# A new table of planned times for the first three units, and five small guards moved to GpSimd

## The chip, the cores and the metric

The kernel runs on one core of a Trainium2 chip. Its engines are TensorE (PE in the profile, with its weight loads as PEld), VectorE (DVE), ScalarE (ACT), GpSimd (POOL) and SyncE (SP), which here issues all the DMAs. Each engine works through its own queue strictly in order; between engines there are semaphores. The metric is the device time of one execution in microseconds (us). Before the change three runs took 532.4, 533.78 and 532.07 us, median 532.4.

## The reference

Two stages. Causal attention with a window of 64 positions, per head, and then a gated block with a convolution of three taps over the sequence:

```python
scores = scale * np.matmul(q, k.transpose(0, 1, 3, 2))       # B=8, H=8, S=576, D=64
mask = (rel >= 0) & (rel < window)                           # window = 64
scores = np.where(mask, scores, -1000000000.0)
scores = scores - np.max(scores, axis=-1, keepdims=True)
attn = np.exp(scores)
attn = attn / (np.sum(attn, axis=-1, keepdims=True) + 1e-09)
x = np.matmul(attn, v)                                       # then [B, S, 512]
h = np.maximum(x @ w_in, 0.0)                                # w_in [512, 1024]
for k in range(K):
    conv_out += conv_w[k][None, None, :] * hp[:, k:k + S, :]  # hp: h padded by one row
gate = 1.0 / (1.0 + np.exp(-conv_out))
out = (h * gate) @ w_out                                     # w_out [1024, 512]
```

The weights arrive as 64-bit floats and are turned into 32-bit ones on the chip.

## The kernel before

**Tiling.** The 8 x 576 positions are cut into twelve units of 384. Per unit the attention is worked off in three blocks `b` (scores in `qk`, L346; the windowed maximum in `row_max`, L361, eight instructions at L363; exponents with their sums in `exps`, L373; 1e-9 added to the sums in `guard`, L376; `reciprocal`, L379; `normalise`, L384). Then the weights of a block are transposed: by TensorE (L390) and copied out by ScalarE (L395) in units 0 and 1, by VectorE (L411) and 24 small DMAs (L423) from unit 2 on. `values` (L487) multiplies by v for four groups `c` of two heads into the two PSUM banks `acc`; ScalarE rounds the result to `xh` (L491), VectorE makes the rest `xl` (L494), so that three single-pass products stand for one in full precision.

**The two big products.** Per unit and per chunk `f` of 128 hidden features (eight of them), `mm1` makes h from x: 12 matmuls at L507, into `acc` banks too. ScalarE takes them out (L528), starts the convolution (L534), VectorE adds the two side taps (L541), ScalarE applies the sigmoid (L548), VectorE multiplies (L553), ScalarE rounds to `gh` (L557) and VectorE makes the rest `gl` (L561), for two chunks at a time. `mm2` adds up the output: 3 matmuls at L570 for each of four output banks `po`, so 12 for a chunk.

**Weights.** `weights` (L261) loads the bits of one chunk or of two (L267), and `to_f32` (L244) makes floats of them: ScalarE's absolute value of the high word (L248), a maximum with 2^-15 (L250 on VectorE for the first two chunks of w_in, which come singly; L252 on GpSimd for all others), two VectorE steps with the bits (L253, L255), ScalarE's scaling of the low word (L258), VectorE's addition (L259). Then the high part is copied, by GpSimd for w_in (L276) and by ScalarE for w_out (L274), and VectorE subtracts it (L277, into `wil` and `wol`). There are two buffers, `w240` and `w241` in the rows below; the single chunks lie in the halves of `w240`.

**What sets the order.** The whole program is a list of pieces of work, each with a planned time: `START` (L140) holds the numbers, counted in chunks (unit 0's first chunk is 0, the attention before it has negative numbers). For `qk`, `ex`, `pv` and `sig` the first row is used around unit 0, the second around unit 1, the third for all later units. `queued` (L61) walks through the list with a cost for each piece and puts onto each engine, at each step, that ready piece whose planned time is lowest. The order it finds is the order in which the instructions are issued. Where it finds TensorE without work it puts in matmuls on a spare tile (`keep_busy`, L207, at L212), a fixed number of them.

Of the kernel before, what the change touches and what calls it, by code (L numbers as in the profile page):

```python
# [12 lines left out]
ALU = mybir.AluOpType  # L13
# [20 lines left out]
TINY = 2.0 ** -15  # L34
# [26 lines left out]
def queued(works, fill=None):  # L61
# [76 lines left out]


START = {  # L140
    "v0": -27.5,
    "pv0": -15.968,
    "conv": -37.437,
    "bits": ((-46.561, -47.419), (-44.383, -45.007)),
    "qk1": -43.011,
    "v1": -11.849,
    "qk2": -2.185,
    "qk0": (-91.154, -52.794, -48.024),
    "ex0": (-42.377, -37.771, -19.993),
    "sc1": (-20.012, -18.408, -14.041),  # L150
    "ex1": (-8.106, -4.046, -3.778),
    "mask": -0.529,
    "sig": ((3.087, 7.079, 8.764, 10.751), (3.178, 6.73, 5.945, 9.966), (4.046, 6.806, 8.285, 10.314)),
    "in": (-39.031, -37.38, -33.878, -12.682, -12.013),
    "out": (-11.963, -8.679, 1.926, 7.315),
# [3 lines left out]
}  # L159
SWITCH = {"PE": 0.14, "ACT": 1.28}  # L160
LEAVE = 0.24
PORT_CL = 0.5
# [5 lines left out]
def attention_moe(ctx: ExitStack, tc: tile.TileContext, q, k, v, w_in, conv_w, w_out, out):  # L168
    nc = tc.nc
# [13 lines left out]
    mask = many(3, [P, P], F32, "mask")  # L183
# [13 lines left out]
    bits = [flat.bitcast(U32)[:, 4 * DM * i:4 * DM * (i + 1)].rearrange("p (e two) -> p e two", two=2) for i in range(2)]  # L197
# [20 lines left out]
    def at(t, eng, cost, do, r=(), w=(), kind=None, mb=0, port=0.0):  # L218

        plan.append(Work(t, eng, cost, do, list(r), list(w), kind, mb, port))  # L220

    def two(t, eng, cost, do, **kw):
        at(t, eng, cost, do, port=cost, **kw)
# [17 lines left out]

    def to_f32(t, n, st, x, kb, kt, early=False):  # L244

        lw, hw, xu = st[..., 0], st[..., 1], x.bitcast(U32)

        at(t, "ACT", 0.0009 * n + 0.2, lambda: nc.scalar.activation(x, hw.bitcast(F32), AF.Abs), r=kb, w=kt)  # L248
        if early:
            two(t, "DVE", 0.00052 * n + 0.06, lambda: nc.vector.tensor_scalar(x, x, TINY, None, op0=ALU.max), w=kt)  # L250
        else:
            at(t, "POOL", 0.0027 * n + 0.02, lambda: nc.gpsimd.tensor_scalar(x, x, TINY, None, op0=ALU.max), w=kt, port=PORT_CL)  # L252
        two(t, "DVE", 0.00052 * n + 0.06, lambda: nc.vector.tensor_scalar(  # L253
            xu, xu, 3, 0x3FFFFFF8, op0=ALU.logical_shift_left, op1=ALU.bitwise_and), w=kt)
        two(t, "DVE", 0.00104 * n + 0.07, lambda: nc.vector.scalar_tensor_tensor(  # L255
            xu, hw, 0xC0000000, xu, op0=ALU.bitwise_and, op1=ALU.bitwise_or), r=kb, w=kt)

        at(t, "ACT", 0.0009 * n + 0.2, lambda: nc.scalar.activation(lw, lw, AF.Copy, scale=2.0 ** -29), w=kb)  # L258
        two(t, "DVE", 0.00104 * n + 0.07, lambda: nc.vector.tensor_tensor(xu, xu, lw, ALU.add), r=kb, w=kt)  # L259

    def weights(t, src, fs, hi, lo, key, buf, halves):  # L261

        e = slice(halves[0] * DM, (halves[-1] + 1) * DM)
        st, x = bits[buf][:, e], w24[buf][:, e]
# [3 lines left out]
                bits[buf][:, a * DM:(a + 1) * DM], src[f].bitcast(U32).rearrange("p (e two) -> p e two", two=2)),  # L268
               w=[("bits", buf, a)], mb=0.52)
        n = len(fs) * DM  # L270
        to_f32(t, n, st, x, kb, kt, len(fs) == 1)
        his, los = [f"{key}{f}h" for f in fs], [f"{key}{f}l" for f in fs]
        if key == "out":
            at(t, "ACT", 0.0009 * n + 0.12, lambda: nc.scalar.copy(hi, x), r=kt, w=his)  # L274
# [159 lines left out]
    def softmax(u, b, t, ex_at):  # L434
# [7 lines left out]
        t = ex_at  # L442
# [2 lines left out]
               w=[("s", b, i), ("sm", b, i)], kind="exp")  # L445
        t += 0.45
        sw = [("sm", b, i) for i in range(NB)]
        if 0 < u < 3:
            at(t, "POOL", 0.6, lambda b=b: guard(b, nc.gpsimd), w=sw)
        else:  # L450
            at(t, "DVE", 0.15, lambda b=b: guard(b, nc.vector), w=sw)
# [285 lines left out]
```

## Time and profile before

| | us |
|---|---|
| median of three runs | 532.4 |
| lowest and highest | 532.07, 533.78 |
| the profiled execution | 530.72 |
| its span on the core | 528.9 |
| first product into the output banks (L570) starts at | 69.49 |
| last matmul group on the chain (L570) ends at | 524.92 |

The profiled execution was 1.7 us faster than the median of the runs. Its span begins with the first instruction and ends with the last one; 1.8 us of the execution lie outside of it. In rows of the timeline the first number is the start in us from the span's start, the second the length, then engine, line, operation, what is written from what, the shapes and the count; in brackets stands how long the engine was idle before it, and what ended that. The granted clock of TensorE was 0.999 of full speed.

### The profile page before, as it was taken

How to read it: one execution, taken by the hardware profiler on the slowest of the kernel's cores; microseconds unless marked ns; L12 is line 12 of the kernel's file. 1: busy time of each engine (PE TensorE's matmuls, PEld its weight loads, DVE VectorE, ACT ScalarE, POOL GpSimd, SP SyncE). 2: the span in 40 equal slices, each digit the busy share in tenths (PEclk: the TensorE clock that was granted, in tenths of full speed). 3: DMA queues.
4: the chain of work that ended last, by engine and by line, in shares of the span. 5: the costliest groups of instructions: out<-in, count | busy, mean ns of one | idle time of the engine just before them, and what ended most of it. 6: DMA issues, size and time to landing. Idle time of an engine off the chain costs nothing.

```text
span 528.9 us, 14823 instructions
## 1 busy us (share of the span) xinstructions
PE 518.7 (98%) x5824; PEld 499.8 (94%) x5824; DVE 376.7 (71%) x1089; ACT 382.1 (72%) x1015; POOL 96.9 (18%) x187
## 2 busy tenths in 40 slices
PE   9999799999999999999999999999999999999996
PEld 8898799999899999999999999999999999999996
DVE  4899999964958677667767767767767667655552
ACT  2999889549896696696697687687687687544542
POOL 5253452103031011021021021021021021000000
PEclk9999999999999999999999999999999999999999
DMA  8992570235283273172182174183074053010011
GB/s 281 352 318 100 195 277 23 68 122 198 75 314 81 78 252 78 48 289 74 26 295 71 24 245 122 27 287 99 14 270 118 14 150 103 20 61 0 2 60 62
DMA packets 29462, 69.98 MB, mean 132 GB/s; under 512 B 5712, under 2 KB 17616, under 8 KB 29392
## 3 DMA queue, kind: packets, MB, share of 16 engines
q1 hardware_dynamic: 29392, 69.03, 39.4%
q8 instruction: 46, 0.75, 0.6%
q14 instruction: 24, 0.20, 0.1%
HBM read 47.73 MB, written 9.47 MB: 108 GB/s over the span
## 4 chain that ended last, share of the span: by engine, by line
PE 87%; DVE 7%; DMA 2%; SPq 1%; ACT 1%; issue 0%; POOL 0%; DVEq 0%
PE po L570 39%; PE acc L507 36%; PE acc L487 6%; PE sc L356 5%; DVE s L384 1%; DMA T<-in_w_in_dram 1%; DVE s L363 1%; SPq L234 1%; DMA q<-in_q_dram 1%; DVE c L541 1%; DVE w L259 1%; DVE wil L277 1%; DVE w L255 1%; ACT s L373 0%; PE po L212 0%
## 5 line engine op out<-in xcount | busy, mean ns | idle before, releaser
L570 PE MATMUL po<-gh,woh 128*128 128x386 f32 (+1 forms) x384 | 132.3, 345 | 0.0
L507 PE MATMUL acc<-xh,wih 128*128 128x384 f32 x384 | 131.5, 342 | 0.6 <-POOL s L439 0.5
L541 DVE SCALAR_TENSOR_TENSOR c<-hbuf,cw,c 128x386 f32<-128x386 f32 (+1 forms) x192 | 109.2, 620 | 32.0 <-ACT c L534 32.0
L570 PE MATMUL po<-gh,wol 128*128 128x386 f32 (+1 forms) x384 | 129.9, 338 | 0.0
L507 PE MATMUL acc<-xh,wil 128*128 128x384 f32 x384 | 129.9, 338 | 0.0
L570 PE MATMUL po<-gl,woh 128*128 128x386 f32 (+1 forms) x384 | 129.9, 338 | 0.0
L507 PE MATMUL acc<-xl,wih 128*128 128x384 f32 x384 | 129.6, 338 | 0.0
L373 ACT ACTIVATE s<-s,nm 128x96 f32<-128x96 f32 (+2 forms) x288 | 105.4, 371 | 5.8 <-DVE nm L363 5.6
L561 DVE TENSOR_TENSOR gl<-c,gh 128x772 fp32r<-128x772 f32 (+1 forms) x48 | 54.9, 1145 | 28.7 <-ACT gh L557 28.5
L570 PEld LDWEIGHTS po<-gh,woh 128*128 128x128 f32 x384 | 72.3, 188 | 2.7
L507 PEld LDWEIGHTS acc<-xh,wih 128*128 128x128 f32 x384 | 72.2, 188 | 2.6 <-POOL s L439 0.7
L570 PEld LDWEIGHTS po<-gl,woh 128*128 128x128 f32 x384 | 72.4, 189 | 0.3 <-DVE gl L561 0.3
L570 PEld LDWEIGHTS po<-gh,wol 128*128 128x128 f32 x384 | 72.3, 188 | 0.0
L507 PEld LDWEIGHTS acc<-xh,wil 128*128 128x128 f32 x384 | 72.2, 188 | 0.0
L553 DVE TENSOR_TENSOR c<-c,hbuf 128x772 f32<-128x772 f32 (+1 forms) x48 | 47.3, 985 | 35.0 <-ACT c L548 35.0
L507 PEld LDWEIGHTS acc<-xl,wih 128*128 128x128 f32 x384 | 72.2, 188 | 0.0
L384 POOL TENSOR_TENSOR s<-s,r 128x768 f32<-128x768 f32 x27 | 39.7, 1471 | 169.9 <-DVE r L379 169.9
L548 ACT ACTIVATE c<-c 128x772 f32<-128x772 f32 (+1 forms) x48 | 40.7, 849 | 32.9 <-DVE c L541 32.7
L528 ACT ACTIVATE hbuf<-acc 128x384 f32<-128x384 f32 x64 | 30.9, 483 | 40.2 <-PE acc L507 40.1
L363 DVE CUSTOM_DVE_ANT_0 s<-sc,mask 128x96 f32<-128x96 f32 (+2 forms) x272 | 51.6, 254 | 11.1 <-PE sc L356 11.0
L373 ACT ACTIVATION_READ_ACCUMULATOR s<-s,nm 128x1 f32 x288 | 55.5, 193 | 0.0
L534 ACT ACTIVATE c<-hbuf,cw 128x386 f32<-128x386 f32 (+1 forms) x96 | 53.6, 609 | 0.9 <-DVE gl L561 0.9
(65 smaller groups left out, 594.1 us busy)
## 6 DMA issues: line engine op xcount, KB each, us to landing
v<-in_v_dram SPq DMA_DIRECT2D x24, 768.0 KB, 7.1
ub<-T SPq DMA_DIRECT2D x240, 48.0 KB, 1.9
k<-in_k_dram SPq DMA_DIRECT2D x22, 448.0 KB, 6.3
q<-in_q_dram SPq DMA_DIRECT2D x22, 384.0 KB, 7.4
out_dram<-T SPq DMA_DIRECT2D x8, 772.0 KB, 4.3
T<-in_w_in_dram SPq DMA_DIRECT2D x8, 512.0 KB, 6.5
T<-in_w_out_dram SPq DMA_DIRECT2D x8, 512.0 KB, 5.1
out_dram<-T SPq DMA_DIRECT2D x3, 768.0 KB, 6.5
```

The source lines that it names most:

```text
L363: nc.vector.tensor_tensor_reduce(out=ss[b][:, i, h, o:n], in0=banks_of(u, b)[h][:, i * P + o:i * P + n], in1=mask[m][:, o:n], scale=-0.125 ...
L373: nc.scalar.activation(x, x, AF.Exp, bias=nms[b][:, e], scale=-1.0, accum_out=sms[b][:, e])
L384: on.tensor_tensor(sv, sv, rs[b].unsqueeze(2).broadcast_to([P, 2 * NB, n]), ALU.mult)
L487: nc.tensor.matmul(acc[bank(("v", u, c))][h * D:(h + 1) * D, t * W:(t + 1) * W], vs[:, c, t, h], ub[g][:, 2 * p:2 * p + 2, 2 * t + h], sta ...
L507: nc.tensor.matmul(acc[bank(("m", u, f))][:, :NX], w[:, f, c], x[u % 2][:, c], start=(c == 0 and j == 0), stop=(c == NC - 1 and j == 2))
L528: nc.scalar.activation(hbuf[:, f, o:o + NX], ps[:, :NX], AF.Relu)
L534: nc.scalar.activation(cs[i % 2][:, a, :n], hbuf[:, f, 1:1 + n], AF.Copy, scale=cw[:, 1, f:f + 1])
L541: nc.vector.scalar_tensor_tensor(c, hbuf[:, f, e:e + n], cw[:, e, f:f + 1], c, op0=ALU.mult, op1=ALU.add)
L548: nc.scalar.activation(c, c, AF.Sigmoid)
L553: nc.vector.tensor_tensor(c, c, hbuf[:, 2 * i:2 * i + 2, 1:1 + n], ALU.mult)
L561: nc.vector.tensor_tensor(gls[ring(u, i)][:, :, :n], cs[i % 2][:, :, :n], ghs[ring(u, i)][:, :, :n].bitcast(F32), ALU.subtract)
L570: nc.tensor.matmul(po[o][:, :n], w[:, f, es], x, start=(f == 0 and j == 0), stop=(f == NF - 1 and j == 2))
```

## The change

Three things are changed. The numbers of `START` are others for everything that belongs to the first three units and to the weights; the rows for later units (the third row of `sig`, `pv`, `ex`, `qk`) stay. The maximum at L250 is gone: the first two chunks of w_in take the GpSimd instruction of L252 as all the others do. And the guards of unit 0's three sums go from VectorE to GpSimd, where those of units 1 and 2 are already. `queued`, its costs and all instructions otherwise stay as they are.

```diff
 START = {
-    "v0": -27.5,
-    "pv0": -15.968,
...
-    "bits": ((-46.561, -47.419), (-44.383, -45.007)),
...
-    "ex0": (-42.377, -37.771, -19.993),
...
+    "v0": -34.213,
+    "pv0": -15.486,
...
+    "bits": ((-44.162, -48.108), (-49.962, -46.523)),
...
+    "ex0": (-38.484, -35.539, -25.91),
...
 }
...
-    def to_f32(t, n, st, x, kb, kt, early=False):
+    def to_f32(t, n, st, x, kb, kt):
...
-        if early:
-            two(t, "DVE", 0.00052 * n + 0.06, lambda: nc.vector.tensor_scalar(x, x, TINY, None, op0=ALU.max), w=kt)
-        else:
-            at(t, "POOL", 0.0027 * n + 0.02, lambda: nc.gpsimd.tensor_scalar(x, x, TINY, None, op0=ALU.max), w=kt, port=PORT_CL)
+        at(t, "POOL", 0.0027 * n + 0.02, lambda: nc.gpsimd.tensor_scalar(x, x, TINY, None, op0=ALU.max), w=kt, port=PORT_CL)
...
-        to_f32(t, n, st, x, kb, kt, len(fs) == 1)
+        to_f32(t, n, st, x, kb, kt)
...
-        if 0 < u < 3:
+        if u < 3:
             at(t, "POOL", 0.6, lambda b=b: guard(b, nc.gpsimd), w=sw)
```

In the changed program every line from L252 on has a number that is 3 lower (L253 becomes L250, L570 becomes L567). Below, the text uses the numbers of before throughout; only the rows of the changed program have its own.

Two places of the order matter. **The first is the first weights, some 13 us into the program.** On VectorE, behind the last maxima of unit 0, stood before:

```order
L250 TENSOR_SCALAR w240_101<-w240_101 128x512
L253 TENSOR_SCALAR w240_101<-w240_101 128x512
L255 SCALAR_TENSOR_TENSOR w240_101<-T_100,w240_101 128x512
L376 TENSOR_SCALAR sm0_86<-sm0_86 128x8
L379 RECIPROCAL r0_89<-sm0_86 128x8
L384 TENSOR_TENSOR s0_80<-s0_80,r0_89 128x1024
L259 ISA w240_101<-T_100,w240_101 128x1024
L277 TENSOR_TENSOR wil_69<-w240_101,wih_68 128x512
```

Now VectorE has there:

```order
L250 TENSOR_SCALAR w240_101<-w240_101 128x512
L252 SCALAR_TENSOR_TENSOR w240_101<-T_100,w240_101 128x512
L376 RECIPROCAL r0_89<-sm0_86 128x8
L381 TENSOR_TENSOR s0_80<-s0_80,r0_89 128x1024
L250 TENSOR_SCALAR w240_101<-w240_101 128x512
L256 ISA w240_101<-T_100,w240_101 128x1024
L252 SCALAR_TENSOR_TENSOR w240_101<-T_100,w240_101 128x512
```

The maximum (L250 of before) and the guard (L376 of before) are gone from VectorE, and the second single chunk begins between the steps of the first. On ScalarE, around the scaling of the low words of chunks 2 and 3 (the 128x1024 row that writes T), stood before:

```order
L491 CAST xh0_63<-acc0_106 128x384
L491 CAST xh0_63<-acc1_107 128x384
L373 ACTIVATE s0_80,sm0_86<-s0_80,nm0_83 128x128 x6
L258 ACTIVATE T_100<-T_100 128x1024
L373 ACTIVATE s0_80,sm0_86<-s0_80,nm0_83 128x64 x2
L248 ACTIVATE cw_72<-cbits_103 128x24
```

Now ScalarE has there:

```order
L248 ACTIVATE w240_101<-T_100 128x1024
L488 CAST xh0_63<-acc0_106 128x384
L488 CAST xh0_63<-acc1_107 128x384
L370 ACTIVATE s0_80,sm0_86<-s0_80,nm0_83 128x128 x4
L255 ACTIVATE T_100<-T_100 128x1024
```

The absolute values of chunks 4 and 5 (L248 into w240) now stand ahead of that scaling; before they stood five rows behind it.

**The second place is ahead of the first product into the output banks.** On VectorE stood before, behind the last of the eight maxima of a block of unit 2 (s1):

```order
L363 ISA s1_81,nm1_84<-sc1_105,mask1_74 128x96
L363 ISA nm1_84 128x1
L561 TENSOR_TENSOR gl0_97<-c0_92,gh0_94 128x772
L259 ISA w240_101<-T_100,w240_101 128x2048
L253 TENSOR_SCALAR w241_102<-w241_102 128x1024
L494 TENSOR_TENSOR xl1_66<-acc0_106,xh1_64 128x384
L255 SCALAR_TENSOR_TENSOR w241_102<-T_100,w241_102 128x1024
L277 TENSOR_TENSOR wol_71<-w240_101,woh_70 128x1024
```

Now VectorE has there:

```order
L252 SCALAR_TENSOR_TENSOR w240_101<-T_100,w240_101 128x1024
L491 TENSOR_TENSOR xl1_66<-acc0_106,xh1_64 128x384
L491 TENSOR_TENSOR xl1_66<-acc1_107,xh1_64 128x384
L558 TENSOR_TENSOR gl0_97<-c0_92,gh0_94 128x772
L256 ISA w240_101<-T_100,w240_101 128x2048
L250 TENSOR_SCALAR w241_102<-w241_102 128x1024
L491 TENSOR_TENSOR xl1_66<-acc0_106,xh1_64 128x384
L252 SCALAR_TENSOR_TENSOR w241_102<-T_100,w241_102 128x1024
L274 TENSOR_TENSOR wol_71<-w240_101,woh_70 128x1024
L360 ISA s1_81,nm1_84<-sc0_104,mask1_74 128x96
```

The maxima of s1 have moved from ahead of `gl0` to behind the first `wol`, and one more `xl` of unit 1 stands ahead. On TensorE stood before:

```order
L487 MATMUL acc1_107<-ub1_62,v_79 64x64 x12
L212 MATMUL po2_110<-spare_112 128x112 x2
L487 MATMUL acc0_106<-ub0_61,v_79 64x64 x12
L212 MATMUL po2_110<-spare_112 128x112 x6
L570 MATMUL po0_108<-gh0_94,woh_70 128x386
```

Now TensorE has there, with nine more rows of L504 (twelve in all) ahead of the first L567:

```order
L212 MATMUL po3_111<-spare_112 128x112 x2
L484 MATMUL acc0_106<-ub1_62,v_79 64x64 x12
L504 MATMUL acc1_107<-xh0_63,wih_68 128x384
L504 MATMUL acc1_107<-xh0_63,wil_69 128x384
L504 MATMUL acc1_107<-xl0_65,wih_68 128x384
```

Twelve matmuls of `mm1` (chunk 6 of unit 0) now stand ahead of the first output product; before they stood behind it. One block of scores (L356, 32 matmuls) which stood ahead of it now stands behind it. Up to there TensorE has 84 matmuls of L507 where it had 72, three of the 32-matmul blocks of scores where it had four, and 99 spare matmuls where it had 104; a profile shows two records for each spare matmul and each one of the scores.

More of the change, by code (lines that the diff above doesn't have):

```diff
@@ L140 @@
 START = {
-    "v0": -27.5,
-    "pv0": -15.968,
-    "conv": -37.437,
-    "bits": ((-46.561, -47.419), (-44.383, -45.007)),
[L145 to L148, printed above, removed]
-    "ex0": (-42.377, -37.771, -19.993),
[L150 to L155, printed above, removed]
[3 rows of a table removed]
+    "v0": -34.213,
+    "pv0": -15.486,
+    "conv": -34.622,
+    "bits": ((-44.162, -48.108), (-49.962, -46.523)),
+    "qk1": -44.058,
+    "v1": -6.318,
+    "qk2": 0.918,
+    "qk0": (-88.698, -55.197, -55.435),
+    "ex0": (-38.484, -35.539, -25.91),
+    "sc1": (-35.664, -14.916, -14.661),
+    "ex1": (-10.948, -3.722, -2.234),
+    "mask": -13.894,
+    "sig": ((5.143, 6.743, 8.637, 10.624), (2.954, 4.077, 7.59, 9.996), (4.046, 6.806, 8.285, 10.314)),
+    "in": (-40.063, -38.679, -33.327, -12.569, -5.818),
+    "out": (-5.241, -4.847, 7.996, 9.148),
[3 rows of a table added]
 }
```

6 rows, old and new, of the table START are left out of this document.

## The prediction

> **What bounds the kernel now.** I read the page's busy times first, then busy time by stretch, then the chain that ended last.
>
> ```profile
> PE 518.7 (98%) x5824; PEld 499.8 (94%) x5824; DVE 376.7 (71%) x1089; ACT 382.1 (72%) x1015; POOL 96.9 (18%) x187
> ```
>
> ```profile
> 10.00:15.00 5.00, 5.00 (x68) 4.83 (x69) 4.17 (x29) 2.80 (x12) 0.09 (x3) 1.00 1.02 409
> ...
> 30.00:35.00 5.00, 5.00 (x87) 4.76 (x92) 5.00 (x22) 4.91 (x20) 3.81 (x4) 1.00 0.99 357
> ...
> 90.00:100.00 10.00, 10.00 (x59) 10.00 (x58) 9.98 (x28) 5.25 (x10) 1.16 (x2) 1.00 0.28 71
> ```
>
> In a stretch's row stand its length, then the busy us of PE, PEld, DVE, ACT and POOL, the clock, and the DMA's share and GB/s. At 30 to 35 us VectorE and ScalarE are both full, and at 90 to 100 VectorE still is. TensorE looks full too, but early on part of that is the spare matmuls:
>
> ```profile
> L212 PE MATMUL acc<-spare 128*128 128x112 f32 x102 | 15.0, 310 | 1.0 <-DVE spare L215 1.0
> L212 PE MATMUL po<-spare 128*128 128x112 f32 x106 | 14.0, 281 | 0.0
> ```
>
> That is 29.0 us of no use, all of it before 69.5 us. The chain of waits says when TensorE takes over (start, length, what):
>
> ```profile
> 15.73 1.23 DVE s L384
> 69.72 3.70 PE po L570 x21
> 84.56 8.44 PE acc L507 x48
> 512.23 12.69 PE po L570 x72
> 525.34 0.32 ACT T L602
> ```
>
> Up to some 56 us its longest pieces are VectorE's; from 69.7 us it is TensorE without a gap worth naming. So the end is **the time at which the first L570 starts, plus TensorE's work left then**. A matmul of L507 or L570 takes a slot of 8.44 / 48 = 0.176 us. What stands just ahead of that start:
>
> ```profile
> 64.89 0.99 PE L356 MATMUL sc<-k,q 64*32 64x96 f32 x64 [1.14 <-DMA q<-in_q_dram]
> ...
> 67.28 0.92 PE L487 MATMUL acc<-ub,v 128*64 128x64 f32 x24
> 68.13 1.59 PE L212 MATMUL po<-spare 128*128 128x112 f32 x12
> 69.49 0.42 PE L570 MATMUL po<-gh,woh 128*128 128x386 f32 x1
> ```
>
> ```profile
> 59.63 0.55 DVE L494 TENSOR_TENSOR xl<-acc,xh 128x384 fp32r<-128x384 f32 x1
> 60.10 1.21 DVE L255 SCALAR_TENSOR_TENSOR w<-T,w 128x1024 uint32<-128x1024 uint32 x1
> 61.23 0.25 DVE L363 CUSTOM_DVE_ANT_0 s<-sc,mask 128x96 f32<-128x96 f32 x1
> ...
> 62.66 0.95 DVE L561 TENSOR_TENSOR gl<-c,gh 128x772 fp32r<-128x772 f32 x1
> ...
> 66.87 1.21 DVE L277 TENSOR_TENSOR wol<-w,woh 128x1024 fp32r<-128x1024 f32 x1
> ```
>
> The first product needs `gl` (63.6) and `wol` (68.1), both from VectorE; the spare matmuls of 68.13 then hold TensorE until 69.5. VectorE's queue sets this start.
>
> **The sum, step one: VectorE's queue, same work.** What goes:
>
> ```profile
> 12.91 0.43 DVE L250 TENSOR_SCALAR w<-w 128x512 f32<-128x512 f32 x1
> ...
> 15.22 0.17 DVE L376 TENSOR_SCALAR sm<-sm 128x8 f32<-128x8 f32 x1 [0.69 <-ACT s L373]
> ...
> 18.27 0.69 DVE L277 TENSOR_TENSOR wil<-w,wih 128x512 fp32r<-128x512 f32 x1 [0.71 <-POOL wih L276]
> 18.88 0.17 DVE L376 TENSOR_SCALAR sm<-sm 128x8 f32<-128x8 f32 x1
> ...
> 26.53 0.58 DVE L376 TENSOR_SCALAR sm<-sm 128x8 f32<-128x8 f32 x1
> ```
>
> Two maxima at 0.43 are 0.9 us, the three guards 0.17 + 0.17 + 0.58 = 0.9. The two waits of 0.69 and 0.71 go as well, 1.4, since other work stands there now. Gone: 3.2 us.
>
> What comes is waiting. GpSimd's rows for the maximum, and the moment at which ScalarE has the first chunk ready:
>
> ```profile
> L252 POOL TENSOR_SCALAR w<-w x7: 2767/2776/3287, 21.4 to 80.4; 128x1024 f32<-128x1024 f32 x7
> L252 POOL TENSOR_SCALAR cw<-cw x1: 268/268/268, 31.8 to 31.8; 128x24 f32<-128x24 f32 x1
> ```
>
> ```profile
> 12.20 0.68 ACT L248 ACTIVATE w<-T 128x512 f32<-128x512 f32 x1 [3.85 <-DMA T<-in_w_in_dram]
> ...
> 28.84 1.20 ACT L258 ACTIVATE T<-T 128x1024 uint32<-128x1024 uint32 x1
> ...
> 32.15 1.17 ACT L248 ACTIVATE w<-T 128x1024 f32<-128x1024 f32 x1
> ```
>
> ```profile
> 30.43 1.21 DVE L259 CUSTOM_DVE_ANT_0 w<-T,w 128x2048 uint16<-128x2048 uint16 x1
> ```
>
> A 512-wide maximum is not in the trace; between 0.27 us for 24 columns and 2.77 for 1024 a straight line gives 1.5. It runs from 12.9 to 14.4, and VectorE, free at 12.9, waits 1.5 us with all maxima done. The lower bound is 0.27, the upper 2.77; I take the line. Queued behind that L253 are the L384 of s0 and with it TensorE's transposes, which slip by about as much; a block of unit 1's scores has been put ahead of them and fills part of that. The bits do not come too late: ScalarE now takes chunk 1 first, whose load is second in the queue as chunk 0's was; chunk 0's is now fourth, two loads of 512 KB behind, at 409 GB/s 1.3 us each, so 14.8, and ScalarE turns to it when the first exponents end, at 15.1. Their guard then runs on GpSimd, beside VectorE's L255; 0.2 for the hop. Next, **ScalarE is as full as VectorE**, and loses no work. It has one L248 more (1.17 us, 0.1 of it beside its neighbour) ahead of the scaling for chunks 2 and 3, which ends at 30.04 now and at 31.1 or later then. VectorE waits for it at L259, which it reached at 30.43 and would reach at about 30.1. I take 1.2; behind it stands the block of maxima of s2 in unit 1. Added waits: 1.5 + 0.2 + 1.2 = 2.9.
>
> Then VectorE and GpSimd hinder each other:
>
> ```profile
> 38.40 2.79 POOL L252 TENSOR_SCALAR w<-w 128x1024 f32<-128x1024 f32 x1 [1.40 <-ACT w L248]
> ```
>
> ```profile
> 32.14 0.96 DVE L253 TENSOR_SCALAR cw<-cw 128x24 uint32<-128x24 uint32 x1
> ...
> 38.48 2.06 DVE L384 TENSOR_TENSOR s<-s,r 128x1024 f32<-128x1024 f32 x1
> ...
> 40.77 1.23 DVE L384 TENSOR_TENSOR s<-s,r 128x1024 f32<-128x1024 f32 x1
> ```
>
> An L384 that starts 0.08 us behind a GpSimd instruction takes 2.06 us in place of 1.23: 0.8 lost. The 24-column L253 loses about as much. Both stand beside other work after the change, and I count them as gone, 1.6; in their place comes the first L384 at 15.9, right behind the second 512-wide maximum (ScalarE has its input ready at 15.1 + 0.7): 0.8 again. So 0.8 gained. Of the five instructions that GpSimd newly runs, each could cost VectorE 0.8 or nothing; that is the range of this term, from 4.0 lost to 1.6 gained.
>
> Together 3.2 - 2.9 + 0.8 = 1.1; with the hops uncertain I take **0.8 us earlier for the same work**.
>
> **Step two: the first L570.** The block of maxima ahead of `gl` leaves, 62.66 - 61.23 = 1.43 us, and one `xl` comes, 60.10 - 59.63 = 0.47. So `wol` is done at 68.08 - 0.8 - 1.43 + 0.47 = 66.3. But TensorE now has more to do there: the last `xl` ahead of `wol` frees a bank for `values` about 2.3 us before that (L255 and L277, 1.21 each less 0.07 of overlap), at 64.0; then 0.85 for `values` and 12 x 0.176 = 2.1 for chunk 6 give 67.1 with the hops. TensorE, no longer VectorE, is last at this place: **67.1 in place of 69.49, 2.4 us earlier**. The spare matmuls (99 in place of 104, 1.2 us fewer) lie ahead of that and are in it. Behind it TensorE has 12 matmuls less (2.1) and one block of scores more (0.99): 1.1 earlier. That makes 3.5.
>
> **Step three: what is late next.** The other `wol` and `gl` must keep up. To the fourth pair of chunks TensorE has 72 L570, 90 L507 and one block of scores, 29.5 us, so it comes at 96.6. VectorE's fourth `wol`:
>
> ```profile
> 90.41 0.95 DVE L561 TENSOR_TENSOR gl<-c,gh 128x772 fp32r<-128x772 f32 x1
> ...
> 92.62 1.21 DVE L277 TENSOR_TENSOR wol<-w,woh 128x1024 fp32r<-128x1024 f32 x1
> 93.75 1.14 DVE L541 SCALAR_TENSOR_TENSOR c<-hbuf,cw,c 128x386 f32<-128x386 f32 x2
> ```
>
> Before, it was ready at 93.83. After, 0.8 earlier, but behind four more L541 (1.14 for two) and one more L561 (0.95), 3.0 with their overlaps, so at 96.0 and with the hop 96.2. The margin is 0.4 us, and at the third pair about 1. I take 1.0 us lost at these places. ScalarE switches its tables twice more there (the first switch of the kind):
>
> ```profile
> 51.64 1.28 ACT L548 ACT_TABLE_LOAD   x1
> 57.14 0.85 ACT L548 ACTIVATE c<-c 128x772 f32<-128x772 f32 x1 [2.61 <-DVE c L541]
> ```
>
> I cost these 2.6 us at nothing: the idle 2.61 us in front of the second sigmoid goes, since exponents stand there now, and from 90 to 100 us ScalarE is half idle (5.25 of 10). Without this cover each costs up to 1.28. Later units' own table entries stay, and TensorE is full there.
>
> So 3.5 - 1.0 = 2.5 us. The profiled execution took 530.7 us and would take 528.2. The median of the runs is 532.4, 1.7 above it; the same 2.5 off that gives **529.9**.
>
> **Rivals.** First, *ScalarE keeps the pace*: what VectorE saves it waits away, so step one gives 0, and one table load shows. That is 2.5 - 0.8 - 1.3 = 0.4 faster, 532.0. For it speaks ScalarE's 4.91 of 5.00 at 30 to 35 us; against it that 2.61 us of idleness at 57 which the new order fills.
>
> Second, *nothing is lost in step three*: 3.5 faster, 528.9. For it: TensorE's margins come out positive; against it: the smallest is 0.4.
>
> Third, *GpSimd holds VectorE for a whole instruction*, and the kernel is slower. The places are the three L384 that would start beside a maximum: at 15.9 behind a 512-wide one (0.7 more than the 0.8 counted), at 22.6 beside a 1024-wide one (2.8), and at about 40 within another (1.9 left of it). Step one falls by 5.4, everything behind it moves along, and 2.5 faster becomes 2.9 slower: 535.3. It decides from a loss of 2.5 us on. For it speaks the L253 row, 0.96 us for 24 columns. Against it speak the two rows of L384: at 38.48 it was done at 40.54 while GpSimd ran until 41.19, and the one at 40.77 took its plain 1.23 inside that same instruction.
>
> The Trainium skill, page "SBUF — State Buffer", section "Who interferes with whom", has this third way as a rule: a VectorE instruction with two SBUF inputs and a GpSimd instruction that reads SBUF lock each other out for the whole instruction. By that rule the kernel would take about the 535.3 of this rival, and the L384 of 38.48 would have begun at 41.19; the trace shows it done by 40.54, so it bears out a delay, not the whole of it.
>
> **How the numbers follow.** Forecast, 1.6 to 3.5 us faster: 0.44. More than that: 0.14. ScalarE keeps the pace, within 1.6 either way: 0.28. GpSimd in the way, slower: 0.14. About 0.3%, 1.6 us, is what a measurement of this kernel can tell from no change. So faster 0.58, same 0.28, slower 0.14. The range goes down to 527.8, which is 1.1 below the second rival, for collisions that do not happen (1.6 in step one, less a part taken by TensorE); up to 533.7, which leaves out the whole lock but takes in the worst of the 0.8 us collisions: 4.0 lost for 0.8 gained is 4.8 less in step one, 2.3 slower by itself, of which I include 1.3, since five in five are unlikely.
>
> **What would show it.** Right: the first L570 between 66.5 and 68; VectorE idle some 1.5 us at 12.9, waiting for GpSimd, and about 1 us before the L259 of chunks 2 and 3, waiting for ScalarE; no wait of TensorE over 1 us between 68 and 110. Step one is wrong if that L259 ends later than 33.5 or an L384 takes over 2.1 us. Step three is wrong if TensorE waits for `gl` or `wol` at 87 or 97 us. The forecast falls if the first L570 starts after 69.

## The result, and the profile after

The changed kernel took 527.57 us (median of five runs, 526.9 to 528.11), the kernel before beside it 532.07 (530.06 to 533.78): ratio 0.9923, 95% interval 0.9905 to 0.9942, so 3 to 5 us faster. A second comparison gave 527.93 against 531.35, ratio 0.9945 (0.9927 to 0.9963). The profiled execution took 527.46 us after 530.72, which is 3.3 less.

The first lines are the engines' busy times on the page of the changed kernel, and busy time in the three stretches shown of before (length; busy us of PE, PEld, DVE, ACT, POOL; clock; DMA share, GB/s).

```profile
PE 516.8 (98%) x5814; PEld 499.1 (95%) x5814; DVE 377.9 (72%) x1084; ACT 384.7 (73%) x1017; POOL 105.2 (20%) x192
```

```profile
10.00:15.00 5.00, 5.00 (x68) 4.72 (x68) 3.72 (x34) 2.75 (x12) 1.58 (x4) 1.00 1.02 402
30.00:35.00 5.00, 4.83 (x84) 4.48 (x91) 5.00 (x22) 5.00 (x22) 3.81 (x5) 1.00 0.88 315
90.00:100.00 10.00, 10.00 (x59) 10.00 (x58) 10.00 (x15) 7.37 (x11) 1.44 (x4) 1.00 0.23 59
```

GpSimd has 8.3 us more, VectorE is as full as before from 30 us on, and nearly half of ScalarE's idle time at 90 to 100 us is filled. In the chain of waits (start, length, what) the hand-over from VectorE to TensorE now lies at the last `xl`:

```profile
50.77 1.84 DVE c L538 x2
...
64.08 0.47 DVE xl L491
64.55 0.04 issue
64.60 0.92 PE acc L484 x24
65.51 2.30 PE acc L504 x12
67.81 2.64 PE po L567 x15
...
508.64 12.70 PE po L567 x72
```

The timeline of TensorE and of VectorE around it:

```profile
60.48 0.92 PE L484 MATMUL acc<-ub,v 128*64 128x64 f32 x24
...
63.55 0.59 PE L212 MATMUL po<-spare 128*128 128x112 f32 x4
64.60 0.92 PE L484 MATMUL acc<-ub,v 128*64 128x64 f32 x24 [0.46 <-DVE xl L491]
...
67.65 0.34 PE L567 MATMUL po<-gh,woh 128*128 128x386 f32 x1
```

```profile
60.76 1.05 DVE L558 TENSOR_TENSOR gl<-c,gh 128x772 fp32r<-128x772 f32 x1
61.73 1.21 DVE L256 CUSTOM_DVE_ANT_0 w<-T,w 128x2048 uint16<-128x2048 uint16 x1
62.87 1.21 DVE L250 TENSOR_SCALAR w<-w 128x1024 uint32<-128x1024 uint32 x1
64.00 0.54 DVE L491 TENSOR_TENSOR xl<-acc,xh 128x384 fp32r<-128x384 f32 x1
...
65.59 1.21 DVE L274 TENSOR_TENSOR wol<-w,woh 128x1024 fp32r<-128x1024 f32 x1
...
95.54 1.22 DVE L274 TENSOR_TENSOR wol<-w,woh 128x1024 fp32r<-128x1024 f32 x1
```

The first product (L567, L570 of before) starts at 67.65 in place of 69.49, 1.84 earlier. `wol` is done at 66.80; TensorE, which had waited 0.46 us for `xl`, is last there. The last group of matmuls starts at 508.64 in place of 512.23, 3.59 earlier, so 1.75 of it were won behind the first product.

### The profile page after: what moved, and what is told of

Its sections match the earlier page's. It is cut to its first block, busy times and chain, and to the rows that moved or that the text cites. A ratio compares the mean times of both kernels' runs of the same rounds, so it can differ in the third digit from the quotient of the medians.

```text
span 525.6 us, 14814 instructions
## 1 busy us (share of the span) xinstructions
PE 516.8 (98%) x5814; PEld 499.1 (95%) x5814; DVE 377.9 (72%) x1084; ACT 384.7 (73%) x1017; POOL 105.2 (20%) x192
## 4 chain that ended last, share of the span: by engine, by line
PE 90%; DVE 8%; issue 1%; ACT 0%
PE po L567 39%; PE acc L504 36%; PE acc L484 6%; PE sc L353 5%; PE acc L212 3%; DVE s L360 1%; DVE c L538 1%; DVE w L256 1%; DVE w L252 1%; DVE wil L274 1%; DVE s L381 1%; DVE w L250 1%; DVE xl L491 1%; PE po L353 0%; DVE cw L252 0%
## 5 line engine op out<-in xcount | busy, mean ns | idle before, releaser
L538 DVE SCALAR_TENSOR_TENSOR c<-hbuf,cw,c 128x386 f32<-128x386 f32 (+1 forms) x192 | 110.0, 624 | 32.9 <-ACT c L531 32.7
L567 PE MATMUL po<-gh,woh 128*128 128x386 f32 (+1 forms) x384 | 132.4, 345 | 0.0
L504 PE MATMUL acc<-xh,wih 128*128 128x384 f32 x384 | 131.1, 341 | 0.8 <-POOL sm L373 0.8
L567 PE MATMUL po<-gh,wol 128*128 128x386 f32 (+1 forms) x384 | 129.8, 338 | 0.0
L567 PE MATMUL po<-gl,woh 128*128 128x386 f32 (+1 forms) x384 | 129.8, 338 | 0.0
L504 PE MATMUL acc<-xh,wil 128*128 128x384 f32 x384 | 129.8, 338 | 0.0
L504 PE MATMUL acc<-xl,wih 128*128 128x384 f32 x384 | 129.7, 338 | 0.0
L567 PEld LDWEIGHTS po<-gh,woh 128*128 128x128 f32 x384 | 72.2, 188 | 2.9
L504 PEld LDWEIGHTS acc<-xh,wih 128*128 128x128 f32 x384 | 72.1, 188 | 2.4 <-POOL sm L373 1.0
L381 POOL TENSOR_TENSOR s<-s,r 128x768 f32<-128x768 f32 x27 | 39.7, 1471 | 165.6 <-DVE r L376 154.3
L567 PEld LDWEIGHTS po<-gl,woh 128*128 128x128 f32 x384 | 72.3, 188 | 0.0
L567 PEld LDWEIGHTS po<-gh,wol 128*128 128x128 f32 x384 | 72.3, 188 | 0.0
L504 PEld LDWEIGHTS acc<-xh,wil 128*128 128x128 f32 x384 | 72.2, 188 | 0.0
L504 PEld LDWEIGHTS acc<-xl,wih 128*128 128x128 f32 x384 | 72.1, 188 | 0.0
```

Source lines behind the costliest of these rows:

```text
L381: on.tensor_tensor(sv, sv, rs[b].unsqueeze(2).broadcast_to([P, 2 * NB, n]), ALU.mult)
L504: nc.tensor.matmul(acc[bank(("m", u, f))][:, :NX], w[:, f, c], x[u % 2][:, c], start=(c == 0 and j == 0), stop=(c == NC - 1 and j == 2))
L538: nc.vector.scalar_tensor_tensor(c, hbuf[:, f, e:e + n], cw[:, e, f:f + 1], c, op0=ALU.mult, op1=ALU.add)
L567: nc.tensor.matmul(po[o][:, :n], w[:, f, es], x, start=(f == 0 and j == 0), stop=(f == NF - 1 and j == 2))
```

## Experiments

**A measuring stick.** Runs of one kernel differ by 2 us and more, so three moments of each profile are compared. M is the start of the second 1024-wide `wil` on VectorE; up to there all orders hold the same VectorE work, but for the five instructions that went to GpSimd. F is the start of the first product, E that of the last group of 72 matmuls on the chain. These rows of before and of the changed kernel give M:

```profile
45.17 1.22 DVE L277 TENSOR_TENSOR wil<-w,wih 128x1024 fp32r<-128x1024 f32 x1
```

```profile
45.02 1.22 DVE L274 TENSOR_TENSOR wil<-w,wih 128x1024 fp32r<-128x1024 f32 x1
```

Two profiles of before, in rows one and two, and two of the changed kernel, in rows three and four, then the experiments (us; the ratio is that to before in the same comparison):

| kernel | median | ratio, interval | M | F - M | E - M |
|---|---|---|---|---|---|
| before | 532.07 | | 45.17 | 24.32 | 467.06 |
| before again | 531.41 | 1.0001 (0.9986, 1.0015) | 45.13 | 23.83 | 466.55 |
| changed | 527.57 | 0.9923 (0.9905, 0.9942) | 45.02 | 22.63 | 463.62 |
| changed again | 527.93 | 0.9945 (0.9927, 0.9963) | 45.46 | 22.63 | 463.69 |
| changed, five instructions back on VectorE | 527.85 | 0.9945 (0.9929, 0.9962) | 45.63 | 22.63 | 463.37 |
| before, five instructions on GpSimd | 531.62 | 1.0005 (0.9993, 1.0017) | 45.87 | 23.87 | 466.61 |
| before, 12 spare rows less | 530.86 | 0.9996 (0.9983, 1.0008) | 45.68 | 22.13 | 466.38 |
| before, block of scores behind | 531.66 | 1.0001 (0.999, 1.0011) | 45.19 | 23.63 | 467.62 |
| before, maxima of s2 first | 529.67 | 0.9978 (0.9958, 0.9997) | 44.74 | 22.15 | 465.54 |
| changed, maxima of s2 behind | 530.09 | 0.9966 (0.9951, 0.998) | 44.99 | 23.96 | 464.90 |
| changed, maxima of s1 ahead of `gl` | 528.84 | 0.9954 (0.994, 0.9969) | 46.00 | 23.44 | 464.20 |
| changed, 12 matmuls behind | 529.13 | 0.9969 (0.9954, 0.9984) | 45.48 | 20.42 | 464.80 |
| changed, one `xl` earlier | 527.32 | 0.9931 (0.9914, 0.9947) | 45.76 | 21.74 | 462.84 |
| changed, path sorted | 527.29 | 0.9923 (0.9906, 0.994) | 46.64 | 21.72 | 462.96 |

All medians of before in these comparisons lie between 531.26 and 532.07. On average M differs little between the orders; among the profiles of one order it differs by up to 1.65 (46.64 and 44.99). E - M of one kernel repeats to 0.1 us for the changed one and to 0.5 for before, where the wait for q differs by as much (1.14 and 0.64 us). What the new order gains is in E - M: 466.8 on average before, 463.65 after, 3.15 less. E - M ends at the last group; from there to the end of the execution the fourteen profiles take 18.4 to 19.1 us.

**Engines or order?** First the changed order with the old engines, then the old order with the new ones.

```diff
-        to_f32(t, n, st, x, kb, kt)
+        to_f32(t, n, st, x, kb, kt, nc.vector if len(fs) == 1 else nc.gpsimd)
...
-            at(t, "POOL", 0.6, lambda b=b: guard(b, nc.gpsimd), w=sw)
+            at(t, "POOL", 0.6, lambda b=b: guard(b, nc.gpsimd if u else nc.vector), w=sw)
```

> The changed kernel with its order of work as it is, but the two 512-wide maxima and unit 0's three guards issued on VectorE again. My theory: the gain comes from the new order, and the five moved instructions are worth about nothing, because what VectorE saves there (0.9 + 0.9 us) it spends waiting for GpSimd (1.00 and 0.13 us) and in the first L381 rows. Then the time is 527.1 to 528.5 us against 527.6 for the changed kernel, and the first product into the output banks starts at 67.0 to 68.3. Rival: the moved instructions carry a good part of the gain; then 529 us or more, the first product at 68.5 or later.

527.85, and E - M 463.37: as the theory has it. The converse, in before:

```diff
-            two(t, "DVE", 0.00052 * n + 0.06, lambda: nc.vector.tensor_scalar(x, x, TINY, None, op0=ALU.max), w=kt)
+            two(t, "DVE", 0.00052 * n + 0.06, lambda: nc.gpsimd.tensor_scalar(x, x, TINY, None, op0=ALU.max), w=kt)
...
-            at(t, "DVE", 0.15, lambda b=b: guard(b, nc.vector), w=sw)
+            at(t, "DVE", 0.15, lambda b=b: guard(b, nc.vector if u else nc.gpsimd), w=sw)
```

> The kernel of before with its order of work as it is, but the two 512-wide maxima and unit 0's three guards issued on GpSimd, as in the change. My theory (the order carries the gain): within 0.8 us of before, 531.3 to 532.9, the first product into the output banks at 69 to 70. VectorE waits about 1.1 us for each of the two maxima there. Rival (the engines carry the gain): 2 us or more faster than before, 530 or less.

531.62, ratio 1.0005. Of the two waits for GpSimd that it expected only the first came, 1.22 us. The five moved instructions are worth nothing that these runs can tell. The order is the change.

**Is it the start of the first product?** In before, the last spare matmuls ahead of it were left out (in `keep_busy`, the 16th group).

```diff
-            for _ in range(n):
+            for _ in range(0 if last else n):
```

> The kernel of before without the last group of spare matmuls (12 rows at 68.13 us, 1.59 us), which stands right ahead of the first product into the output banks. My theory: the start of that product sets the end, and wol is ready at 68.08, so the product starts at 68.1 to 68.3 in place of 69.5 and the kernel is 1.1 to 1.4 us faster than before. Rival one: the time is lost again behind it, because gl and wol of the next chunks then come late (TensorE waits for VectorE at the second to fourth pair); less than 0.5 us faster. Rival two: the spare matmuls hold the granted clock up and their lack costs more than it brings; slower.

Rival one. The first matmul started at 67.81, and the second waited for `wol` at once (in this kernel each line has a number 4 higher than in before):

```profile
64.57 0.99 PE L360 MATMUL sc<-k,q 64*32 64x96 f32 x64 [0.32 <-DMA q<-in_q_dram]
...
67.81 0.44 PE L574 MATMUL po<-gh,woh 128*128 128x386 f32 x1
68.64 0.44 PE L574 MATMUL po<-gh,wol 128*128 128x386 f32 x1 [0.38 <-DVE wol L281]
```

The spare matmuls stood in time that TensorE would have waited anyway. The same question in the changed kernel: its 12 matmuls of `mm1` (chunk 7) ahead of the first product were moved behind its first 12. (The description of the order and the prediction call them chunk 6; that one stands behind the first product. The count is the same.) Here and below, whole pieces of work are moved in the list behind `queued`, and `find` picks a piece by its function and its unit.

```diff
+    xs = find(works, "mm1", u=0, f=7)
+    for x in xs:
+        works.remove(x)
+    n = works.index(find(works, "mm2", u=0, f=0, o=3)[0]) + 1
+    works[n:n] = xs
```

> The changed kernel, with the 12 matmuls of mm1 that stand right ahead of the first product (2.1 us) moved behind the first 12 of the output product. Theory (what counts is TensorE's idle and spare time ahead of the first product, not when that product starts): the first product starts at about 66.9 when wol is ready, 0.8 earlier, but TensorE idles some 1.4 us ahead of it and has 2.1 us more to do behind it, so 1.0 to 1.4 us slower than the changed kernel, about 528.8. Rival (the start of the first product sets the end): 0.5 to 0.8 us faster.

```profile
65.90 0.44 PE L567 MATMUL po<-gh,woh 128*128 128x386 f32 x1
67.32 0.44 PE L567 MATMUL po<-gh,wol 128*128 128x386 f32 x1 [0.98 <-DVE wol L274]
```

The first matmul of the product started 2.2 us earlier (F - M 20.42), the next ones waited for `wol`, and the end came 1.15 later. So the theory holds: what counts is useful work in the time in which VectorE makes TensorE wait, not the moment at which the product starts.

**What the places on VectorE are worth.** The block of maxima of s1 back ahead of the first `gl`:

```diff
+    x = find(works, "row_max", u=2, b=1)[0]
+    works.remove(x)
+    works.insert(works.index(find(works, "gate_lo", u=0, i=0)[0]), x)
```

> The changed kernel, with the block of eight row maxima of unit 2 (s1, 1.43 us of VectorE) put back ahead of the first gl, where it stood before. Theory (VectorE's queue is what TensorE waits for ahead of the first product, so each us there is a us at the end): xl of group 0, wol and the first product 1.4 us later (about 69.0), the time 1.1 to 1.5 us more than the changed kernel, about 528.9. Rival (VectorE's place there is worth nothing, because it was the wait for q that was removed): within 0.4 us of the changed kernel.

F - M rose by 0.81 and E - M by 0.55; the median is 0.9 above that of the changed kernel beside it. The direction is the theory's, the size half of it: the block costs 1.43, but the L250 that took 1.21 in the changed kernel beside GpSimd lost nothing at its new time.

Then the wait for q, which stands in the old order ahead of the first product:

```diff
+    x = find(works, "qk", u=3, b=2)[0]
+    works.remove(x)
+    works.insert(works.index(find(works, "mm2", u=0, f=0, o=3)[0]) + 1, x)
```

> The kernel of before, with the one block of scores of unit 3 that waits for q ahead of the first product (0.99 us at 64.89) moved behind the first 12 matmuls of the output product; nothing else. Theory (this wait, 0.32 to 1.14 us in four profiles, and the block itself hold TensorE up, and wol is right behind): the first product starts at 68.1 to 68.4, when wol is ready, 0.6 to 1.3 us earlier than in the two profiles of before, and 0.99 us more stand behind it, so 0 to 0.4 us faster: 531.0 to 531.5 against 531.4. Rival (the wait for q is what made before slow and is worth its whole length and more): 1 us or more faster, 530.4 or less.

531.66 against 531.69, ratio 1.0001: without the wait nothing is gained that these runs can tell. `wol` is ready no earlier (68.10), and the block (0.99) then stands behind.

```profile
60.67 1.26 PE L212 MATMUL po<-spare 128*128 128x112 f32 x10
```

The first product started at 68.82, later than expected, but this profile is no measure of it. From 55 to 60 us the granted clock was 0.66, where it was 1.00 in before, and the spare matmuls of this row, which start at 59.22 in before, came 1.45 us later. So the finding rests on the medians, and F - M and E - M of this run are not to be compared with the others.

**An exchange at 51 us.** The VectorE rows of the two orders, before first, show where the same work takes less time:

```profile
50.84 3.77 DVE L541 SCALAR_TENSOR_TENSOR c<-hbuf,cw,c 128x386 f32<-128x386 f32 x4
...
55.96 1.14 DVE L541 SCALAR_TENSOR_TENSOR c<-hbuf,cw,c 128x386 f32<-128x386 f32 x2
57.02 1.21 DVE L277 TENSOR_TENSOR wil<-w,wih 128x1024 fp32r<-128x1024 f32 x1
```

```profile
50.68 1.93 DVE L538 SCALAR_TENSOR_TENSOR c<-hbuf,cw,c 128x386 f32<-128x386 f32 x2
...
53.95 1.14 DVE L538 SCALAR_TENSOR_TENSOR c<-hbuf,cw,c 128x386 f32<-128x386 f32 x2
55.02 1.21 DVE L274 TENSOR_TENSOR wil<-w,wih 128x1024 fp32r<-128x1024 f32 x1
56.16 1.14 DVE L538 SCALAR_TENSOR_TENSOR c<-hbuf,cw,c 128x386 f32<-128x386 f32 x2
```

Between the pairs stand the eight maxima of s2, behind four L541 in the old order and behind two in the new. GpSimd's maximum starts at 52.33 and 52.17. The six took 3.77 + 1.14 = 4.91 us, and 1.93 + 1.14 + 1.14 = 4.21 after. The exchange was undone in the changed kernel and made alone in before:

```diff
+    x = find(works, "row_max", u=2, b=2)[0]
+    works.remove(x)
+    works.insert(works.index(find(works, "conv_side", u=0, i=1, e=0)[0]) + 1, x)
```

> The changed kernel, with the maxima of unit 2's block s2 (eight rows at 52.53) behind the next two L538 instead of ahead of them, as in the order of before. Theory (most of what VectorE gains for the same work ahead of wol is won here, not at the first weights: four L541 in a row beside GpSimd's maximum took 3.77 us before, two and two with the row maxima between them took 1.93 + 1.14 now, while at 47.5 us the two orders stood 0.15 us apart): the first gl starts 0.6 to 0.8 us later (61.4 to 62.0), and the time is 0.5 to 0.8 us more than the changed kernel, about 528.4. Rival (the gain came from the first weights): no change, within 0.3 us.

```profile
55.73 1.16 PE L353 MATMUL sc<-k,q 64*32 64x96 f32 x64 [2.62 <-DVE nm L360]
...
68.95 0.34 PE L567 MATMUL po<-gh,woh 128*128 128x386 f32 x1
```

It costs 1.3 us (F - M and E - M alike), more than expected: the maxima hold two PSUM banks, and TensorE's next scores waited 2.62 us for them; in the changed kernel they start at 53.91. The median, 530.09, is 2.2 above that of the changed kernel in another comparison (1.1 by the two ratios to before), but its profiled execution is the fastest of its ten runs, of which six had a lower granted clock (below). The converse:

```diff
+    x = find(works, "row_max", u=2, b=2)[0]
+    works.remove(x)
+    works.insert(works.index(find(works, "conv_side", u=0, i=1, e=0)[0]), x)
```

> The converse in the kernel of before: the maxima of unit 2's block s2 ahead of the second pair of L541 instead of behind it; nothing else. Theory (this one exchange frees VectorE of a collision with GpSimd's maximum and TensorE's next scores and values from their wait for the maxima): wil (57.02 us) starts 0.7 to 0.8 us earlier, TensorE's scores of s1 start at 54.2 in place of 55.92, the load of q behind them is issued as much earlier and no longer waited for, the first product starts at 67.7 to 68.3 in place of 69.0 to 69.5, and the time is 0.8 to 1.4 us less than before, 530.1 to 530.7. Rival (the exchange is worth nothing without the new order behind it): within 0.4 us of before, as when the block of scores was moved.

```profile
50.41 1.93 DVE L541 SCALAR_TENSOR_TENSOR c<-hbuf,cw,c 128x386 f32<-128x386 f32 x2
53.68 2.20 DVE L541 SCALAR_TENSOR_TENSOR c<-hbuf,cw,c 128x386 f32<-128x386 f32 x4
55.81 1.21 DVE L277 TENSOR_TENSOR wil<-w,wih 128x1024 fp32r<-128x1024 f32 x1
```

```profile
53.80 1.00 PE L356 MATMUL sc<-k,q 64*32 64x96 f32 x64
...
62.28 1.00 PE L356 MATMUL sc<-k,q 64*32 64x96 f32 x64
66.89 0.42 PE L570 MATMUL po<-gh,woh 128*128 128x386 f32 x1
```

One block of eight instructions moved by two places takes 1.6 us off before (529.67 against 531.26; the interval of the ratio goes from 0.2 to 2.2 us), E - M 1.0 to 1.5. Without the collision four L541 take 2.20 us; the scores start at 53.80, the load of q that follows them is in time, and no wait is left at 62.28.

**Can more be had?** TensorE's path to the first product in the changed kernel starts at an `xl` that stands behind an L250. It was put ahead, and the 4 spare rows at 63.55 were left out:

```diff
+    x = find(works, "split_lo", u=1, c=0)[0]
+    dve = [y for y in works if y.eng == "DVE"]
+    y = dve[dve.index(x) - 1]
+    works.remove(y)
+    works.insert(works.index(x) + 1, y)
...
+    works.remove(y)
```

> The changed kernel, with one xl (of group 0, 0.54 us) put ahead of the shift of L250 at 62.87 that stood in front of it, and without the 4 rows of spare matmuls at 63.55. Theory (the xl frees a bank for the last values, and these with the 12 matmuls behind them are TensorE's path to the first product): the values start at 63.6 in place of 64.6, the matmuls end at 66.6, and wol (66.8) is last; the first product at 66.9 and the time 0.5 to 0.8 us less than the changed kernel, about 526.9. Rival one (the pairs behind have no margin left, gl and wol come late there): less than 0.2 us. Rival two: L250 then meets GpSimd's clearing at another place and wol comes later by as much.

F - M is 0.89 less and E - M 0.8; the median 527.32 is 0.6 below the changed kernel beside it, and the intervals overlap. Then three such moves on VectorE and one on ScalarE:

```diff
+    ahead(c2, first)
+    ahead(c1, first)
+    ahead(c0, shift)
+    ahead(wol0, second)
...
+    ahead(h5, act[act.index(h5) - 1])
...
+    y.do = keep_busy(8, ("po", 3))
```

> The changed kernel with VectorE's work sorted by what TensorE waits for ahead of the first product: the two xl of groups 2 and 1 ahead of the L252 at 58.69, the xl of group 0 ahead of the L250 at 62.87, wol ahead of the L252 at 64.46; on ScalarE the relu of chunk 5 ahead of the copy to woh; 16 rows of spare matmuls less (12 of the 28 at 57.17, the 4 at 63.55). Theory: values start at 59.3 in place of 60.5, the last values at 63.4, the first product at 66.4 in place of 67.6 (wol is ready at 65.4), 1.2 us earlier; behind it the margins of the second to fourth pair (1.6, 0.8, 0.6 us in the changed kernel's profile) take part of it back unless gh comes earlier too: 0.6 to 1.2 us less than the changed kernel, 526.4 to 527.1. Rival (step three of the prediction: the pairs behind cannot come earlier): TensorE waits for wol at the fourth pair, and the gain is under 0.4 us, 527.3 or more.

527.29; E - M 462.96, no more than the single move gave. TensorE never waited for `gl` or `wol` behind the first product, so the rival's reason falls, though its size is near: the last values waited 1.15 us for the same `xl`, which stands behind L256, and the L252 ahead of that took 1.51 us in place of 1.21:

```profile
61.25 1.51 DVE L252 SCALAR_TENSOR_TENSOR w<-T,w 128x1024 uint32<-128x1024 uint32 x1
...
64.69 0.54 DVE L491 TENSOR_TENSOR xl<-acc,xh 128x384 fp32r<-128x384 f32 x1
```

```profile
65.29 0.92 PE L484 MATMUL acc<-ub,v 128*64 128x64 f32 x24 [1.15 <-DVE xl L491]
```

**The spread of the runs.** Both kernels were run again, before first:

> The kernel of before once more, with a second profile. The runs of before lie between 530.06 and 533.78, and its profiled execution (530.72) near the low end, while the five of the changed kernel lie within 1.2 us. Theory one: the first loads vary from run to run (the first score matmuls wait for q and k), so a second profile shows the first row maximum at another time than 7.31 us and the end moved by as much. Theory two: the start is the same and the difference arises later (a wait in the middle of the attention); then the first maximum is at 7.3 again and the first product into the output banks at another time than 69.49.

> The changed kernel once more, with a second profile, as the measure for the three runs beside it. My theory of the spread: in the three profiles of the old order (before twice, and with the five instructions moved) the last matmul group starts 447.33 to 447.35 us after the block of unit 3's scores that waits for q ahead of the first product, whatever that wait was (0.64 to 1.14 us), so a good part of the old spread of 530 to 533 us is this load's. The new order has no such wait there, so its runs should again lie within about 1.5 us, 526.5 to 528.2, and the second profile should give 527 to 528 with a first product at 67.3 to 68. Rival: the spread has other sources; then this one spreads over 3 us as well.

The first maximum came at 7.82 in place of 7.31, but M at 45.13: the later start was hidden by then, and the difference in E (511.68 after 512.23) is nearly that of the wait for q, as theory two has it, though not its start at 7.3. The changed kernel spread from 526.75 to 531.78, so its expectation failed. A part of this spread arises at the first weights: ScalarE now takes chunk 0 when its load has just landed, without a wait in the first profile, after 0.44 us in the second (M 0.44 later) and after 0.42 us with the path sorted, where the load of chunk 1, which it takes first, came late too (4.76 us of idle, 13.03 in place of 12.24), with M at 46.64.

```profile
13.03 0.68 ACT L248 ACTIVATE w<-T 128x512 f32<-128x512 f32 x1 [4.76 <-DMA T<-in_w_in_dram]
16.44 0.67 ACT L248 ACTIVATE w<-T 128x512 f32<-128x512 f32 x1 [0.42 <-DMA T<-in_w_in_dram]
```

Much of the rest goes with the granted clock, which is known for each of these runs. Of the twelve runs of this second comparison of the changed kernel, eight with 0.998 or more took 526.75 to 529.0 us and four with 0.997 or less 529.78 to 531.78; at 0.998 or more the medians of before and of the changed kernel there are 531.12 and 527.75, 3.4 apart. With the maxima of s2 behind, four runs at 0.999 took 528.28 to 529.16 and six at 0.997 or less 529.73 to 530.87. For before, in four comparisons, the medians are 531.08 (58 runs at 0.998 or more) and 531.96 (35 below), and the two groups overlap. The one profile that shows a low clock ahead of the last group is that of the moved block of scores. What lowers the clock, and what the remaining spread comes from, is open.

## Why the prediction was right, and where it was not

The direction and the main mechanism held; the forecast was 2.5 us less, and 3.3 came in the profiled execution. Of the 2.3 us between the forecast median and the measured one, 0.7 are in the sum (528.2 against 527.46 for the profiled execution). The other 1.6 come from carrying over the distance between profile and median: 1.7 us in before, but 0.1 after. One profiled execution at the fast end of a spread was taken for a constant. The median lies 0.2 below the stated range, 527.8 to 533.7. By the ratios to before it is 4.1 us (first comparison) or 2.9 us (second) faster, on both sides of the 3.5 at which the likeliest case (0.44) ended and a rarer one (0.14) began.

By the terms of the sum, the first product came 1.84 earlier for 2.4, behind it 1.75 were won for 1.1, and step three took nothing for 1.0. That is 3.59 at the last group for 2.5; behind it 0.33 were lost again, within what these profiles differ by there.

**What bounds the kernel.** That VectorE's queue sets the start of the first product was half of it. In before TensorE came to that place at 68.13, as `wol` was ready at 68.08, and the wait for q of 1.14 us, quoted there and not used, was on its path. Taking the wait for q away alone gave nothing.

**Step one** is the step that failed. Its number was right, its place was not: 0.8 us for the same work was forecast at the first weights. At M the two orders are 0.15 us apart in the first pair of profiles, and the other way round by 0.3 in the second; over the six profiles in the old order M is 45.30 on average, over the eight in the new one 45.62. The prediction's own signs of a failure here did not show it: L259 ended at 32.80 (33.5 was the limit), and no L384 took more than 2.06 (2.1). The 512-wide maximum took 1.49 us, as the straight line gave, and VectorE waited 1.00 us for the first one; the wait of 1.2 us for ScalarE at L259 did not come. ScalarE's scaling did end at 31.16, as forecast, but VectorE, which the L381 of 28.68 had kept, came to L259 only at 31.59. In its place came collisions, which the sum had counted as a gain of 0.8:

```profile
16.06 1.52 DVE L381 TENSOR_TENSOR s<-s,r 128x1024 f32<-128x1024 f32 x1
...
23.69 1.52 DVE L274 TENSOR_TENSOR wil<-w,wih 128x512 fp32r<-128x512 f32 x1
...
28.68 2.06 DVE L381 TENSOR_TENSOR s<-s,r 128x1024 f32<-128x1024 f32 x1
...
39.45 1.02 DVE L252 SCALAR_TENSOR_TENSOR cw<-cbits,cw 128x24 uint32<-128x24 uint32 x1
```

Against 1.23, 0.69, 1.23 and 0.17 us without one these lose 0.29 + 0.83 + 0.83 + 0.85 = 2.8, where before lost 1.7 at two. GpSimd's 1024-wide maxima stretched as well, from 2.891 us on average to 3.672. What step one hoped for was won at 51 to 57 us instead, by an exchange that the prediction never priced: `gl` starts 1.90 earlier, of which 1.43 is the block of maxima that left, less 0.47 for the added `xl`, so 0.94 for the same work, and 0.78 of it arise between M and the `wil` at 57.02 (55.02, and 1.07 for the pair that now follows). The exchange also freed TensorE's scores, which the prediction had not linked with it.

**Step two** held: TensorE, not VectorE, is last ahead of the first product, at 67.65 (67.1 forecast), because the bank came free at 64.5 in place of 64.0. That its start is no measure by itself, as the sum assumed by adding the work left, showed well: 12 matmuls back behind it cost 1.15. Behind it 1.75 were won for 1.1 forecast; TensorE has no gap in either trace there. Counted from start to start, the matmuls of the two products took 2.87 us less there, where 12 slots are 2.11: 60 of them in place of 68 took more than 0.2 us, most of these beside matmuls of another shape. The blocks of scores took 1.28 more for 0.99 forecast, those of `values` 0.16 less, which makes up the other 0.6.

**Step three** was too careful. Its margins were right: the fourth `wol` is done at 96.76, TensorE comes there at 97.32, 0.56 later (0.4 forecast). But 1.0 us was then taken off for places whose margin was positive, and no wait came. With 0.8 less in E - M the earlier `xl` shows that these pairs could come earlier still. This term alone makes rival two, 528.9, the nearer case.

**The other rivals.** ScalarE did not keep the pace, and its idle 2.61 us at 57 went, as forecast. GpSimd did not hold VectorE for whole instructions: the L381 of 16.06 began within a GpSimd maximum (15.89 to 17.38) and ended at 17.58, where a lock for the whole instruction would have let it start at 17.38. The Trainium skill, page "SBUF — State Buffer", section "Who interferes with whom", has such a lock as its rule; this row speaks against it where VectorE comes second, and the rows of the last section speak for it where GpSimd does.

**By parts.** Undone one at a time in the changed kernel, the exchange at 51 us costs 1.3 us of E - M, the 12 matmuls 1.15, and the block of s1 0.55. Together that is 3.0 of the 3.15 that separate the two orders; that the three simply add up was not tried.

## What to carry to other kernels

When an order of work changes, compare the moments at which each engine has done the same work, stage by stage, before giving the gain to an edit: here the edits at the start had brought nothing by M, and eight instructions moved by two places brought a third to a half. An engine kept waiting loses by idle time, not by starting a stage late; put useful work there. And where two limits end at one place, as `wol` and the load of q did, removing one of them brought nothing.

## What the runs showed of the hardware

Which of two instructions starts second matters when VectorE and GpSimd meet. In the second profile of the changed kernel a GpSimd maximum that started while VectorE ran an L381 took 2.21 us in place of 1.49, and that L381 took its plain 1.22:

```profile
16.02 2.21 POOL L249 TENSOR_SCALAR w<-w 128x512 f32<-128x512 f32 x1 [0.64 <-ACT w L248]
```

```profile
15.65 1.22 DVE L381 TENSOR_TENSOR s<-s,r 128x1024 f32<-128x1024 f32 x1
```

It ended at 18.23, about when it would have if it had waited for the end of L381 at 16.87. The 1024-wide maxima show the same. These two rows are from the first profile of the changed kernel:

```profile
27.90 3.50 POOL L249 TENSOR_SCALAR w<-w 128x1024 f32<-128x1024 f32 x1 [1.17 <-ACT w L248]
```

```profile
27.54 1.23 DVE L252 SCALAR_TENSOR_TENSOR w<-T,w 128x1024 uint32<-128x1024 uint32 x1
```

The maximum took 0.73 more than its plain 2.77, and L252 ended at 28.77, 0.87 behind the maximum's start. At 16.02 the two figures are 0.72 and 0.85, at 39.27 0.13 and 0.27, at 83.15 0.69 and 0.83. So in these rows GpSimd is held up for the rest of VectorE's instruction, less some 0.14 us. (The maximum at 72.18, which took 6.24, was held up for longer than one.)

The other way round VectorE loses some 0.3 to 0.85 us, and then goes on beside GpSimd. An estimate from these rows says which instruction it is. Taken back by 2.77 from its end at 31.40, the maximum of 27.90 got going at 28.63, and the L381 that started 0.05 behind that lost 0.83; the L381 of 16.06, which started 0.17 behind a 512-wide one, lost 0.29. At the exchange at 51 us the maximum of the new order got going at 52.47 by the same estimate, and a row maximum, which reads its scores from PSUM, starts at 52.53 and takes its plain 0.24; in the old order the L541 go on there. That this is what the exchange saves on VectorE fits the rows, but was not tried by itself. An L538 pair well inside GpSimd's maximum lost nothing (53.95, 1.14 us).
